# Gate and up of two row blocks as seven block products, in a kernel of a 2D spectral filter and a ReGLU

## The chip, the cores and the metric

The kernel runs on one core of a Trainium2 chip. The metric is the device time of one execution in microseconds; the time before is the median of three runs, 408.8 us (408.67 to 408.9).

## The reference

```python
x = A_x                                        # 1 x 2048 x 512, float32
xn = layernorm(x)                              # over the last axis
s = irfft2(rfft2(xn) * (w_r + 1j * w_i))       # over (2048, 512)
gate, up = xn @ W_gate, xn @ W_up              # 512 x 1376 each
g = silu((relu(gate) * up) @ W_down)           # 1376 x 512
return x + s * g
```

## The kernel before

The 2048 rows lie as 16 tiles of 128 rows by 512. Two tiles make a chunk (c or q from 0 to 7), four a row block (0 to 3); features come as 11 tiles of 128, the last one (TAIL) of 96. Every float32 operand is split into a float16 high and a float16 low part, and every product is three matmuls (PASSES: high by high, high by low, low by high).

The work has two strands. The feed-forward strand: `product` makes gate (i = 0) and up (i = 1) of one feature tile for a row block, 12 matmuls of 128x512 each; `rectify` (ACT) and `hidden` (DVE, ACT, DVE) make the float16 pair h16 from them; `down` multiplies by the down weights `wds`, and `gate` applies silu on ACT. The spectral strand is a DFT in steps: `fold`, `split` and `first_stage` (PE tile s, result through DRAM buffer A_d), then eight `fft_chunk`s (PE tiles y, xx, z, v; DVE multiplies by the filter in `tt`, POOL adds in `po` and `pf`; through DRAM buffer C_d), then `last_stage`. `finish` multiplies s by g, adds x and stores.

At the start `load_x` and `load_group` fetch the first two chunks and the gate and up weights in seven groups (`raw0` to `raw6`; in rows, raw0_0 is gate's and raw0_1 up's). `squares` sums squares of each weight tile on ACT (rows wgu,m<-raw), PE adds them over the partitions (sum, small), DVE makes scales of them (p), and `group_split` makes the float16 pairs `wgu`. Chunks 0 and 1 are normalised to `xf`, transposed on PE (head) and copied to `xT` by ACT (high) and DVE (low). Row block 0's first two features are computed in two halves, so that chunk 0 can begin before chunk 1. The down weights `wds` are scaled by the greatest of all: ACT sums their absolute values (rows wds,md<-wds), DVE takes the maximum `md`, and `greatest` sends it over the partitions by two DMAs on SP (row_md out to DRAM, rows_md back in), after which DVE makes the scales `scd`, and ACT (high) and DVE (low) split each feature's weights. No `down` product can begin before its weights are split.

`keep_busy` gives PE 79 matmuls on ones, without use, at the start. All DMAs are issued by SP. The class `Plan` sets the order on every engine: steps have costs, due times and leads (numbers at the head of the file), and a greedy list of them is written out as the program, each engine running its own in order. Operations are recorded through one helper, so all of them carry its line (L65; in the changed file L81).

## Time and profile before

| | |
|---|---|
| median of three runs | 408.8 us |
| the profiled execution, from first to last instruction | 407.1 us |
| busy: DVE, ACT, POOL | 304.0, 188.0, 46.7 us |
| DMA moved | 51.78 MB |
| the 16 DMA engines' time on the main queue | 42.5% |

The profiled execution's span is 1.7 us below the median of the runs; what lies around the span is not in the trace. Times in the profile count from the span's start. PE is the matmul engine and PEld its weight loads, which overlap the matmuls; DVE, ACT and POOL are the vector, scalar and GpSimd engines; SPq is the queue from which SP issues DMAs.

### The profile page before, as it was taken

The numbers are of one execution on the slowest core, as the hardware profiler recorded it, in microseconds if no ns is written. First come the engines' busy times: TensorE is split into PE (matmuls) and PEld (weight loads), VectorE is DVE, ScalarE is ACT, GpSimd is POOL, SyncE is SP. The second block draws the span as 40 slices with busy tenths as digits, with TensorE's granted clock in tenths as the row PEclk, the third lists the DMA queues.
The fourth block names the chain that finished last, engine by engine and source line by source line (L and its number), as shares of the span: only waits on it lengthen the run. The fifth ranks groups of instructions, "written<-read, shape, count | busy, mean of one in ns | idle before, by whom it ended". The sixth has DMA issues, their size and how long they took to land.

```text
span 407.1 us, 7606 instructions
## 1 busy us (share of the span) xinstructions
PE 401.4 (99%) x2992; PEld 211.5 (52%) x2992; DVE 304.0 (75%) x647; ACT 188.0 (46%) x358; POOL 46.7 (11%) x72
## 2 busy tenths in 40 slices
PE   8999999999999999999999999999999999999995
PEld 7864444444444445455465455546555444444555
DVE  4897986998798979706987578686792328987974
ACT  4999823743467636222355433534523336242411
POOL 0000000000000000001612032030330008040300
PEclk9999999999999999999999999999999999999999
DMA  7980002218549608690006540324201297563242
GB/s 244 403 304 1 0 2 109 54 52 208 171 152 305 172 15 209 128 291 13 2 0 191 173 144 0 100 92 149 52 2 52 61 242 182 161 185 105 103 156 103
DMA packets 36291, 51.78 MB, mean 127 GB/s; under 512 B 15840, under 2 KB 17600, under 8 KB 36256
## 3 DMA queue, kind: packets, MB, share of 16 engines
q1 hardware_dynamic: 36256, 51.31, 42.5%
q8 instruction: 23, 0.38, 0.4%
q14 instruction: 12, 0.10, 0.1%
HBM read 35.55 MB, written 12.60 MB: 118 GB/s over the span
## 4 chain that ended last, share of the span: by engine, by line
PE 97%; ACT 1%; DVE 1%; issue 0%
PE gu L65 55%; PE dn L65 27%; PE s L65 3%; PE z L65 3%; PE xx L65 3%; PE small L65 2%; PE y L65 2%; PE v L65 2%; PE dn_3b L65 1%; ACT xT L65 1%; ACT wgu L65 0%; PE head L65 0%; DVE xT L65 0%; PE sum L65 0%; DVE p L65 0%
## 5 line engine op out<-in xcount | busy, mean ns | idle before, releaser
L65 PE MATMUL gu<-xT,wgu 128*128 128x512 f16 (+1 forms) x1008 | 213.3, 369 | 0.4 <-DVE xT L65 0.4
L65 PEld LDWEIGHTS <-wgu 128*128 128x128 f16 x1008 | 97.5, 98 | 107.5 <-issue 3.5
L65 PE MATMUL dn<-wds,h 128*128 128x512 f16 (+2 forms) x528 | 115.8, 373 | 0.0
L65 PEld LDWEIGHTS <-h 128*128 128x128 f16 (+1 forms) x561 | 53.7, 98 | 57.3 <-issue 2.0
L65 DVE TENSOR_TENSOR h<-gu,r 128x512 f32<-128x512 f32 (+2 forms) x52 | 33.6, 646 | 24.2 <-PE gu L65 22.9
L65 ACT ACTIVATE h<-h 128x512 f16<-128x512 f32 (+1 forms) x44 | 27.5, 626 | 51.0 <-DVE h L65 51.0
L65 POOL TENSOR_TENSOR po<-tt,tt 128x256 f32<-128x256 f32 x16 | 14.4, 900 | 262.6 <-DVE tt L65 208.7
L65 ACT ACTIVATE r<-gu 128x512 f32<-128x512 f32 (+1 forms) x44 | 26.2, 595 | 36.5 <-PE gu L65 36.3
L65 DVE TENSOR_TENSOR h<-h,h 128x512 f16<-128x512 f32 (+1 forms) x44 | 29.7, 689 | 5.3 <-ACT h L65 5.1
L65 DVE SCALAR_TENSOR_TENSOR tt<-xsp,cw,wt 128x512 f32<-128x512 f32 x32 | 25.3, 847 | 0.0
L65 POOL TENSOR_TENSOR ae<-zz 128x128 f32<-128x128 f32 (+1 forms) x32 | 17.8, 593 | 62.8 <-ACT zz L65 47.9
L65 ACT ACTIVATE g<-dn,cdi 128x512 f32<-128x512 f32 (+1 forms) x16 | 10.6, 673 | 23.9 <-PE dn L65 23.9
L65 PE MATMUL gu<-xT,wgt 128*64 128x256 f16 (+1 forms) x144 | 17.0, 309 | 0.0
L65 DVE TENSOR_TENSOR sv<-sv,g 128x512 f32<-128x512 f32 (+1 forms) x17 | 11.2, 690 | 6.4 <-ACT g L65 6.1
L65 DVE TENSOR_TENSOR t<-v,t 128x1024 f16<-128x1024 f32 x8 | 9.8, 1219 | 7.9 <-ACT t L65 7.9
L65 DVE TENSOR_TENSOR z<-z,z 128x1024 f16<-128x1024 f32 x8 | 9.7, 1218 | 7.5 <-ACT z L65 7.5
L65 ACT ACTIVATE z<-z 128x1024 f16<-128x1024 f32 x8 | 8.2, 1024 | 15.2 <-PE z L65 15.2
L65 POOL TENSOR_TENSOR pf<-tt,tt 128x256 f32<-128x256 f32 x16 | 14.0, 888 | 7.7 <-PE gu L65 7.7
L65 ACT ACTIVATE p<-pf 128x1024 f16<-128x1024 f32 x8 | 8.4, 1056 | 13.0 <-DVE pf L65 13.0
L65 DVE SCALAR_TENSOR_TENSOR wgu<-raw,p,wgu 128x512 f16<-128x512 f32 x20 | 14.4, 745 | 0.1
L65 ACT ACTIVATE xs<-xs 128x1024 f16<-128x1024 f32 x8 | 8.3, 1052 | 12.8 <-DVE xs L65 9.3
L65 ACT ACTIVATE wgu<-raw 128x512 f16<-128x512 f32 x20 | 12.3, 619 | 3.7 <-DMA raw<-in_wg 3.7
(134 smaller groups left out, 430.6 us busy)
## 6 DMA issues: line engine op xcount, KB each, us to landing
A_d<-t SPq DMA_DIRECT2D x16, 256.0 KB, 3.3
rw<-in_wl SPq DMA_DIRECT2D x8, 512.0 KB, 5.1
wt<-in_wl SPq DMA_DIRECT2D x8, 512.0 KB, 4.8
at<-A_d SPq DMA_DIRECT2D x8, 512.0 KB, 4.9
C_d<-t SPq DMA_DIRECT2D x16, 256.0 KB, 3.3
ct<-C_d SPq DMA_DIRECT2D x16, 256.0 KB, 5.6
xt<-in_x SPq DMA_DIRECT2D x16, 256.0 KB, 4.3
out<-xt SPq DMA_DIRECT2D x15, 256.0 KB, 2.1
```

Of the source, the lines that this page charges most:

```text
L65: return lambda *args, **kw: self.tc.keep_in_program_order(f(*args, **kw))
```

## The change

Row blocks 2 and 3 take ten of the feature tiles in five pairs (PAIRS). For one pair, the 512 rows are two halves, the 512 inputs two halves, and gate and up are the two columns of a 2 by 2 block product of eight blocks; `fast_products` forms it from seven (Strassen's method, in Winograd's form). One block product is 12 matmuls of 128x256. Three accumulators A, B, C in PSUM (rows sa, sb, sc) take the products; ACT copies partial sums from A to B and from C to `back` (sk), DVE adds `back` and B into C and E (se). The hidden values follow on DVE or POOL. TAIL and blocks 0 and 1 (PLAIN) stay plain products. In all, PE has 432 instead of 912 matmuls of 128x512 for gu, and 840 of 128x256 more.

The operands of the seven products are sums. `row_sums` makes four of the normalised rows for each of the two blocks (POOL or DVE), splits them, writes them to DRAM (S_d), and transposes them back by DMA. `weight_sums` loads each pair's raw weights a second time, scales them on ACT by the kept scales (csc), makes four differences on POOL or DVE, and splits them into `wT`; one of them takes the place of up's low half in `wgu`.

Further: the transposes of chunks 2 to 7 go through DRAM too (X_d); silu's result of blocks 0 to 2 is written out to DRAM (G_d) and read back for `finish`; for chunks 0, 2, 3, 4 and 5 x is copied to the output by a DMA from DRAM to DRAM, and s by g is added to it by an accumulating DMA that POOL issues (ADDS). Statistics of chunk 2 and some normalising move to ACT. PSUM tag gu has three buffers instead of two, dn one instead of two; the pools k4, k2 and xg get smaller. All due times are replaced, and thus the order on every engine.

The diff, cut:

```diff
+PAIRS = ((0, 1), (3, 4), (5, 6), (7, 8), (2, 9))
...
-T0, DOWN, FIRST, FIRST_STEP, MID, MID_STEP, LAST, LAST_STEP = 1.2, 94.9, 53.3, 17.6, 150.3, 18.1, 292.6, 10.8
-LOADS, LOADX = [4.2, 0, 4.4, None, None, None, None], [-2.7, -0.3]
...
+T0, DOWN = 1.2, 72.63
+FIRSTS = [56.77, 70.59, 88.5, 109.16, 99.23, 144.36, 170.4, 200.62]
+LOADS, LOADX = [-28.05, -8.07, -11.28, None, None, None, None], [-2.7, -0.3]
...
+STATS, ADDS, COPIES = ['DVE', 'DVE', 'ACT', 'DVE', 'DVE', 'DVE', 'DVE', 'DVE'], ['DMA', 'DVE', 'DMA', 'DMA', 'DMA', 'DMA', 'DVE', 'DVE'], [200, 200, 200, 200, 200, 130.87, 134.53, 134.53]
-BUSY, LATE, PAIR1, PAIR2 = 79, 0.4, 0, 0
-SQUARES, HALF = 32.82, 2
+BUSY, LATE = 79, 0.4
+SQUARES, HALF = -0.132, 2
...
+ROOM = {"k4": 10, "k2": 8, "kg": 4, "cm": 3, "h16": 11, "xg": 3, "F": 2, "gu": 3, "dn": 1, "q": 4, "q4": 2, "mv": 4, "m": 4, "p": 4, "am": 1, "mid": 3}
+SUMS, TSUMS = ['POOL', 'POOL', 'POOL', 'DVE'], ['DVE', 'POOL', 'DVE', 'POOL', 'POOL']
+TPREP, TSTEP, XLEAD = 108.983, 31.324, 24.245
+PLAIN = {(1, n) for n in range(5)}
...
-    T = Plan({"k4": 12, "k2": 10, "h16": NFT, "xg": NBL + 1, "F": 2, "gu": 2, "dn": 2, "q": 4, "q4": 2, "mv": 4, "m": 4, "p": 4, "am": 1, "mid": 3})
+    T = Plan(ROOM)
...
-            SP.dma_start_transpose(xt.rearrange("p i k r -> p (i k) r"), x16().rearrange("p i h d -> p (i h d)"))
-        step("SP", 3.4, run, reads=[(f"x16_{c}", i, h) for i in range(2) for h in range(2)], 
-             writes=[(f"xT{c // 2}", j, h) for j in range(2 * (c % 2), 2 * (c % 2) + 2) for h in range(2)], kb=100)
+            SP.dma_start_transpose(xt.rearrange("p i k r -> p (i k) r"), X_d[c])
+        step("SP", .6, lambda: SP.dma_start(X_d[c], x16().rearrange("p i h d -> p (i h d)")),
+             reads=[(f"x16_{c}", i, h) for i in range(2) for h in range(2)], writes=[("X_d", c)], kb=512, due=XDUE[c])
+        step("SP", .6, run, reads=[("X_d", c)], writes=[(f"xT{c // 2}", j, h) for j in range(2 * (c % 2), 2 * (c % 2) + 2) for h in range(2)], kb=900, lead=XLEAD)
+    def row_sums(c):
+        xa, xb = (lambda k=k: T[f"xf{2 * c + k}"] for k in range(2))
+        X = [(f"xf{2 * c + k}", i) for k in range(2) for i in range(2)]
+        sx, s16 = ([f"{k}{c}_{a}" for a in range(2)] for k in ("sx", "sx16_"))
+        for a in range(2):
...
+        lo, hi = slice(0, 256), slice(256, 512)
+        eng, e, cost = (DVE, "DVE", dve(512)) if SUMS[c] == "DVE" else (POOL, "POOL", pool(512))
+        S = lambda n: T[sx[n // 2]][:, n % 2]
+        for n, op, a, b, needs in ((0, "tensor_add", lambda: xb()[:, :, lo], lambda: xb()[:, :, hi], []),
+                                   (1, "tensor_sub", lambda: S(0), lambda: xa()[:, :, lo], [(sx[0], 0)]),
+                                   (2, "tensor_sub", lambda: xa()[:, :, lo], lambda: xb()[:, :, lo], []),
+                                   (3, "tensor_sub", lambda: xa()[:, :, hi], lambda: S(1), [(sx[0], 1)])):
+            step(e, cost, lambda n=n, op=op, a=a, b=b: getattr(eng, op)(S(n), a(), b()), reads=X + needs, writes=[(sx[n // 2], n % 2)], port=True)
+        tile_of(f"xS{c}", "xg", [P, 4, 2, 4, P], F16)
+        for a in range(2):
+            halves = [(sx[a], k) for k in range(2)]
+            step("ACT", act(1024), lambda a=a: ACT.activation(T[s16[a]][:, :, :, 0, :], T[sx[a]], AF.Copy), reads=halves, writes=[(s16[a], 0)])
+            step("DVE", dve(1024), lambda a=a: DVE.tensor_sub(T[s16[a]][:, :, :, 1, :], T[sx[a]], T[s16[a]][:, :, :, 0, :]),
+                 reads=halves + [(s16[a], 0)], writes=[(s16[a], 1)], port=True)
...
+            step("SP", .6, lambda a=a, flat=flat: SP.dma_start(S_d[c][a], flat()), reads=[(s16[a], 0), (s16[a], 1)], writes=[("S_d", c, a)], kb=512,
+                 due=SDUE[c])
+            step("SP", .6, run, reads=[("S_d", c, a)], writes=[(f"xS{c}", a)], kb=900, lead=XLEAD)
...
+    def weight_sums(n, due):
+        fs = PAIRS[n]
+        raw, t16 = f"rp{n}", f"wT{n}"
+        tile_of(raw, "xg", [P, 2, 4, 2 * P], F32)
+        for i, src in enumerate((wg, wu)):
+            for j, f in enumerate(fs):
...
+                step("SP", .5, lambda i=i, j=j, of=of, o=o: SP.dma_start(T[raw][:, i, :, j * P:j * P + P], of[:, :, o:o + P]),
+                     reads=["go"], writes=[(raw, i, j)], lead=8, kb=256, due=due - 12)
+                part = lambda i=i, j=j: T[raw][:, i, :, j * P:j * P + P]
+                step("ACT", act(512) + .1, lambda part=part, f=f, i=i: ACT.activation(part(), part(), AF.Copy, scale=csc[:, i, f:f + 1]),
+                     reads=[("csc", f)], writes=[(raw, i, j)])
...
+        minus((0, 0), (1, 0), (0, 0), G + U, t1)
+        minus((1, 0), (1, 1), (1, 0), U + [t1], t3)
+        minus((1, 1), (1, 1), (0, 0), U + [t1, t3], t2)
+        minus((0, 1), (0, 1), (1, 1), G + [t2], t4)
+        for to, of, needs, k in ((slice(0, 2), lambda: T[raw][:, 0].rearrange("p (t k) f -> p t k f", t=2), [t1, t4, t2], 0),
+                                 (slice(2, 3), lambda: B(1, 1).unsqueeze(1), [t2, t4], 2)):
...
+            step("ACT", act(m), lambda to=to, of=of: ACT.activation(wT[n][:, to, 0], of(), AF.Copy), reads=needs, writes=[(t16, k)], due=due + 2)
+            step("DVE", dve(m), lambda to=to, of=of: DVE.tensor_sub(wT[n][:, to, 1], of(), wT[n][:, to, 0]), reads=needs + [(t16, k)], writes=[(t16, k + 1)], port=True, due=due + 4)
+        for j, f in enumerate(fs):
...
+            step("ACT", act(256), lambda to=to, of=of: ACT.activation(to(0), of(), AF.Copy), reads=[t3], writes=[("wgu", f, 0, 1)], due=due + 2)
+            step("DVE", dve(256), lambda to=to, of=of: DVE.tensor_sub(to(1), of(), to(0)), reads=[t3, ("wgu", f, 0, 1)], writes=[("wgu", f, 1, 1)], port=True, due=due + 4)
...
+    def fast_products(c, n):
+        fs = PAIRS[n]
+        A, B, C, back, E, r1, r2 = (f"{k}{c}_{n}" for k in ("sa", "sb", "sc", "sk", "se", "sr", "sq"))
+        for name, tag in ((A, "gu"), (B, "gu"), (C, "gu"), (back, "kg"), (E, "kg"), (r1, "kg"), (r2, "kg")):
+            tile_of(name, tag, [P, 2, 256], F32)
...
+        def mult(to, x, w, fresh, reads):
+            def run():
+                for j in range(2):
+                    for k in range(2):
+                        for p, (h, l) in enumerate(PASSES):
+                            matmul(T[to][:, j, :], w(h, k, j), x(l, k), start=fresh and j == k == p == 0, stop=j == k == 1 and p == 2, skip_group_check=True)
+            step("PE", pe(12, 256), run, reads=reads, writes=[to, "turn"], due=tick(pe(12, 256)))
+        def copy(to, of, due=None):
+            step("ACT", act(512), lambda: ACT.activation(T[to], T[of], AF.Copy), reads=[of], writes=[to], due=due)
+        def add(to):
+            step("DVE", dve(512), lambda: DVE.tensor_add(T[to], T[B], T[back]), reads=[B, back], writes=[to], due=clock[0] + 2)
+        def rect(to, of):
+            step("ACT", act(512), lambda: ACT.activation(T[to], T[of], AF.Relu, scale=2.0 ** -22), reads=[of], writes=[to], due=clock[0] + 3)
+        mult(A, rows(0, 0), plain(0, 0), True, X[0] + W[0])
+        copy(B, A)
+        mult(C, rsum(2), plain(1, 0), True, [(f"xS{c}", 1)] + W[1])
+        copy(back, C)
+        mult(B, rsum(1), summed(2), False, [(f"xS{c}", 0)] + U(2, 3))
+        mult(A, rows(0, 2), plain(0, 2), False, X[0] + W[0])
+        rect(r1, A)
+        add(C)
+        mult(B, rsum(0), summed(0), False, [(f"xS{c}", 0)] + U(0, 1))
+        mult(C, rows(1, 2), summed(1), False, X[1] + U(0, 1))
+        rect(r2, C)
+        add(E)
+        mult(B, rsum(3), plain(1, 2), False, [(f"xS{c}", 1)] + W[1])
+        step("DVE", dve(512), lambda: DVE.tensor_mul(T[r1], T[B], T[r1]), reads=[B], writes=[r1], due=clock[0] + 3)
+        e, eng, cost = (("DVE", DVE, dve), ("POOL", POOL, pool))[SECONDS[5 * c + n] == "POOL"]
+        step(e, cost(512), lambda: eng.tensor_mul(T[E], T[E], T[r2]), reads=[r2], writes=[E], due=clock[0] + 3, port=True)
+        for m, h32 in enumerate((r1, E)):
...
+            step("ACT", act(512), lambda h32=h32, h16=h16: ACT.activation(T[h16][:, 0], T[h32], AF.Copy), reads=[h32], writes=[(h16, 0)])
...
+            step(e, cost(512), lambda h32=h32, h16=h16, eng=eng: eng.tensor_sub(T[h16][:, 1], T[h32], T[h16][:, 0]), reads=[h32, (h16, 0)], writes=[(h16, 1)], port=True)
+    def ff_steps(c, lag=2):
+        for n in range(len(PAIRS)):
+            if (c, n) in PLAIN:
+                for f in PAIRS[n]:
+                    product(c, f, 0)
+                    rectify(c, f)
+                    product(c, f, 1)
+                    hidden(c, f)
+            else:
+                fast_products(c, n)
+            if n >= lag:
+                for f in PAIRS[n - lag]:
+                    down(c, f, 0)
...
+        if b < NBL - 1:
+            tile_of(g, "k2", [P, D], F32)
+            step("SP", .5, lambda: SP.dma_start(T[g], G_d[:, 2 * c + i, :]), reads=[("G_d", b, j), (sn, 2)], writes=[(g, 0)], lead=8, kb=256)
+        if ADDS[c] == "DMA":
+            to = out[:, 2 * c + i, :]
+            step("SP", .5, lambda: SP.dma_start(to, x[:, 2 * c + i, :]), writes=[("out", c, i)], lead=10, kb=512, due=COPIES[c])
+            step("DVE", dve(D), lambda: DVE.tensor_mul(T[sn][:, i, :], T[sn][:, i, :], T[g]), port=True,
+                 reads=[(g, 0), *((sn, k) for k in range(3))], writes=[(sn, 3 + i)])
+            step("POOL", 1.2, lambda: POOL.dma_start(to, T[sn][:, i, :], accum_op=ALU.add), reads=[(sn, 3 + i)], writes=[("out", c, i)], kb=512, lag=3., due=due)
+            return
...
+        for n in range(len(PAIRS)):
+            if (c, n) not in PLAIN and (c == 1 or (c - 1, n) in PLAIN):
+                weight_sums(n, TPREP + n * TSTEP)
         ff_steps(c)
```

What the order shows at three places:

The first is the start. SP's loads before (x0 and x1 are chunks 0 and 1, raw the weights of gate and up, wds those of down):

```order
L65 DMA x0_121<-in_x 128x512 x2
L65 DMA raw0_0_128<-in_wg 128x512
L65 DMA raw0_1_133<-in_wu 128x512
L65 DMA x1_148<-in_x 128x1024
L65 DMA raw1_0_152<-in_wg 128x512
L65 DMA raw1_1_163<-in_wu 128x512
L65 DMA raw2_0_171<-in_wg 128x512
L65 DMA raw2_1_178<-in_wu 128x512
L65 DMA raw3_0_190<-in_wg 128x1024
L65 DMA raw3_1_197<-in_wu 128x1024
L65 DMA wds_85<-in_wd 128x3x512
```

and with the change:

```order
L81 DMA wds_107<-in_wd 128x3x512
L81 DMA raw0_0_145<-in_wg 128x512
L81 DMA raw0_1_149<-in_wu 128x512
L81 DMA x0_153<-in_x 128x512 x2
L81 DMA wds_107<-in_wd 128x3x512
L81 DMA wds_107<-in_wd 128x2x512 x2
L81 DMA x1_200<-in_x 128x1024
L81 DMA raw2_0_216<-in_wg 128x512
L81 DMA raw2_1_224<-in_wu 128x512
L81 DMA raw1_0_207<-in_wg 128x512
L81 DMA raw1_1_249<-in_wu 128x512
L81 DMA raw3_0_256<-in_wg 128x1024
```

The loads of the down weights came after those of x and of four weight groups; now one stands first, and three more ahead of x1. On ACT before, between the first squares and the transposed rows of chunk 0 (xT0):

```order
L65 ACTIVATE wgu0_77,m0_168<-raw0_0_128 128x512
L65 ACTIVATE q0_166<-q0_166 128x2
L65 ACTIVATE wgu0_77,m0_168<-raw0_1_133 128x512
L65 ACTIVATE xf0_201<-x0_121,q0_166 128x512
L65 ACTIVATE wgu0_77<-raw0_0_128,p0_210 128x512
L65 ACTIVATE xT0_233<-head0_214 128x512 x2
L65 ACTIVATE wgu1_78,m1_251<-raw1_0_152 128x512
L65 ACTIVATE wgu1_78,m1_251<-raw1_1_163 128x512
L65 ACTIVATE wgu0_77<-raw0_1_133,p0_210 128x512
```

and with the change:

```order
L81 ACTIVATE wgu0_94,m0_181<-raw0_0_145 128x512
L81 ACTIVATE wgu0_94,m0_181<-raw0_1_149 128x512
L81 ACTIVATE wds_107,md_112<-wds_107 128x512 x2
L81 ACTIVATE q0_229<-q0_229 128x2
L81 ACTIVATE wds_107,md_112<-wds_107 128x512
L81 ACTIVATE wgu0_94<-raw0_0_145,p0_232 128x512
L81 ACTIVATE wgu0_94<-raw0_1_149,p0_232 128x512
L81 ACTIVATE wds_107,md_112<-wds_107 128x512
L81 ACTIVATE xf0_281<-x0_153,q0_229 128x512
L81 ACTIVATE wds_107,md_112<-wds_107 128x512
L81 ACTIVATE xT0_298<-head0_286 128x512 x2
L81 ACTIVATE wds_107,md_112<-wds_107 128x512 x2
```

Five sums over the down weights now stand ahead of xT0, and three more follow ahead of the second chunk's xT0 (not shown).

The second is DVE behind the maximum of the down weights; xs16_1 is the operand of chunk 1's first stage s1_1, which on PE stood ahead of the tail product and now stands among the first down products. Before:

```order
L65 TENSOR_REDUCE max_md_105<-rows_md_104 128x1
L65 TENSOR_SCALAR pd_106<-max_md_105 128x1
L65 TENSOR_SCALAR pd_106<-pd_106 128x1 x2
L65 TENSOR_SCALAR cdi_87<-pd_106 128x1
L65 TENSOR_SCALAR scd_91<-rho_86,pd_106 128x11
L65 TENSOR_TENSOR xs16_1_684<-xs1_570,xs16_1_684 128x2x512
L65 TENSOR_TENSOR h32_0_8_843<-gu0_8_1_803,r0_8_817 128x512
L65 SCALAR_TENSOR_TENSOR wds_85<-wds_85,scd_91 128x512
```

and with the change, from nine rows behind the maximum:

```order
L81 TENSOR_TENSOR h16_0_8_909<-h32_0_8_905,h16_0_8_909 128x512
L81 TENSOR_TENSOR xs1_726<-ee1_718 128x2x65
L81 TENSOR_TENSOR xs1_726<-ee1_718 128x2x64
L81 SCALAR_TENSOR_TENSOR wds_107<-wds_107,scd_114 128x512
L81 TENSOR_TENSOR xs1_726<-ee1_718 128x2x64
L81 TENSOR_TENSOR xs1_726<-ee1_718 128x2x63
L81 TENSOR_SCALAR st2_794<-st2_794 128x2
L81 BN_STATS st3_940<-x3_722 128x6
L81 BN_AGGR mv3_942<-st3_940 128x2
L81 SCALAR_TENSOR_TENSOR wds_107<-wds_107,scd_114 128x512
L81 TENSOR_TENSOR h32_0_9_961<-gu0_9_1_914,r0_9_928 128x512
L81 TENSOR_TENSOR xs16_1_944<-xs1_726,xs16_1_944 128x2x512
```

The low part of xs16_1 came directly behind scd, from sums xs1 made long before; now four of xs1's sums, two splits of down weights and other work stand between.

The third is the first pair of seven products in block 2 (sb2_0 and sc2_0 its accumulators, sk2_0 the copy), on DVE:

```order
L81 SCALAR_TENSOR_TENSOR tt0_0_2516<-xsp_0_2496,cw_110,wt_0_1854 128x512
L81 SCALAR_TENSOR_TENSOR tt1_0_2534<-xsp_0_2496,cw_110,wt_0_1854 128x512
L81 SCALAR_TENSOR_TENSOR tt2_0_2536<-xsp_0_2496,cw_110,wt_0_1854 128x512
L81 SCALAR_TENSOR_TENSOR tt3_0_2553<-xsp_0_2496,cw_110,wt_0_1854 128x512
L81 TENSOR_TENSOR xsp_1_2555<-xx1_2519,xo1_2551 128x256
L81 TENSOR_TENSOR xsp_1_2555<-xx1_2519,xo1_2551 128x4x32
L81 TENSOR_TENSOR xsp_1_2555<-xo1_2551,xx1_2519 128x4x32
L81 SCALAR_TENSOR_TENSOR tt0_1_2577<-xsp_1_2555,cw_110,wt_1_2037 128x512
L81 TENSOR_TENSOR sc2_0_2538<-sb2_0_2532,sk2_0_2574 128x512
L81 COPY zd_138<-zb_2484 128x2
L81 TENSOR_SCALAR zd_138<-zb_2484 128x2
```

The addition into sc2_0, which the next product into sb2_0 waits for, stands behind filter multiplications of spectral chunks 0 and 1.

223 lines of the change are left out of this document (145 added, 78 removed).

## The prediction

> **What bounds the kernel now.** I read the page's busy time first, then the time by stretches of 20 us, then the chain of waits.
>
> ```profile
> PE 401.4 (99%) x2992; PEld 211.5 (52%) x2992; DVE 304.0 (75%) x647; ACT 188.0 (46%) x358; POOL 46.7 (11%) x72
> ```
>
> In the stretches the numbers are the length, then busy time and instructions of PE, PEld, DVE, ACT and POOL, then the granted clock, the DMA engines' share and GB/s:
>
> ```profile
> 0.00:20.00 20.00, 18.78 (x150) 15.67 (x151) 13.22 (x46) 13.55 (x34) 1.00 (x8) 1.00 0.89 322
> 20.00:40.00 20.00, 19.61 (x119) 11.40 (x117) 17.59 (x47) 19.15 (x53) 0.00 (x0) 1.00 0.47 162
> 60.00:80.00 20.00, 20.00 (x152) 9.97 (x151) 15.06 (x30) 10.95 (x18) 0.00 (x0) 1.00 0.26 83
> ```
>
> PE is full from 20 us on; its busy 18.78 us before that hold the useless matmuls on ones. The chain (start, length, what) says the same: from 20.83 on it runs on PE with no other engine between, to 403.03; behind that comes a short tail.
>
> ```profile
> 20.83 18.24 PE gu L65 x107
> ...
> 41.80 0.34 PE sum L65 x4
> ...
> 68.06 1.44 PE s L65 x48
> 69.50 4.13 PE gu L65 x36
> 73.63 27.30 PE dn L65 x126
> ...
> 103.12 15.54 PE gu L65 x72
> ...
> 187.47 1.31 PE xx L65 x12
> ...
> 403.03 0.02 issue
> 403.06 0.48 ACT g L65
> 403.56 0.43 DVE sv L65
> 404.02 0.42 DVE xt L65
> ```
>
> So work taken from PE is worth its full time as long as PE stays fed, and whatever makes PE wait costs its full time. Two things follow: price PE's work, then look for where PE will wait. The tail behind PE keeps its form, since the last block's last products, gate and additions are as before, and counts as zero.
>
> **PE's work.** A 512-wide matmul takes 15.54/72 = 0.216 us, a 256-wide one 1.31/12 = 0.109 us (rows at 103.12 and 187.47). The change takes 480 of the first (103.6 us) and adds 840 of the second (91.7 us): **-11.9 us**. Every row of weight loads speaks for the 0.109:
>
> ```profile
> L65 PEld LDWEIGHTS <-wgu 128*128 128x128 f16 x1008 | 97.5, 98 | 107.5 <-issue 3.5
> ```
>
> 98 ns stay below 109, so a new weight load per 256-wide matmul is still covered, with little left.
>
> **The start.** In the second half of the first features, at 20.83, PE becomes full. What lies ahead of it:
>
> ```profile
> GB/s 244 403 304 1 0 2 109 54 52 208 171 152 305 172 15 209 128 291 13 2 0 191 173 144 0 100 92 149 52 2 52 61 242 182 161 185 105 103 156 103
> ...
> 0.73 0.86 SPq L65 DMA_DIRECT2D x<-in_x  x2
> 3.49 0.69 DVE L65 BATCH_NORM_STATS2 st<-x 128x6 f32<-128x512 f32 x1 [2.47 <-DMA x<-in_x]
> 5.97 0.63 ACT L65 ACTIVATE wgu<-raw 128x512 f16<-128x512 f32 x1 [3.75 <-DMA raw<-in_wg]
> 9.14 0.69 DVE L65 BATCH_NORM_STATS2 st<-x 128x6 f32<-128x512 f32 x1
> 19.49 1.29 DVE L65 TENSOR_TENSOR xT<-head,xT 128x512 f16<-128x512 f32 x2 [0.81 <-ACT xT L65]
> 20.83 11.33 PE L65 MATMUL gu<-xT,wgu 128*128 128x256 f16 x75 [0.39 <-DVE xT L65]
> ```
>
> The first row is the rate in 40 slices of 10.2 us: 2.5 MB by 10.2 us, 6.6 MB by 20.4. x0 landed at 3.5, raw0 at 6.0. In the new order of SP's loads 768 KB of down weights stand ahead of x0, and 1,792 KB more ahead of x1. By these slices the first 2.6 MB (down to the second load of wds) are in at some 10.5 us, x1 (4.2 MB) at 14.4, raw1 at 17.0, raw3 at 19.6. On ACT, which was busy 13.55 us of the first 20 (first stretch) and began its squares at 5.97, stand eight more sums over wds:
>
> ```profile
> L65 ACT ACTIVATE wds<-wds 128x512 f32<-128x512 f32 x10 | 6.2, 617 | 0.0
> L65 ACT ACTIVATE wgu<-raw,p 128x512 f16<-128x512 f32 x12 | 8.1, 714 | 0.6 <-DVE p L65 0.6
> L65 ACT ACTIVATE xf<-x,q 128x512 f32<-128x512 f32 x2 | 1.6, 814 | 0.4 <-DVE q L65 0.4
> L65 ACT ACTIVATE xT<-head 128x512 f16<-128x512 f32 x4 | 2.2, 589 | 0.9 <-PE head L65 0.9
> ```
>
> ACT's row up to the second xT0 is now: 19 squares or sums of 0.62 (11.8 us), four splits of 0.71 (2.8), two xf (1.6), three of four xT0 copies (1.8): 18 us. Without any wait it ends at 24, and DVE's two low copies (1.29) bring PE's second half to 25.1, that is 4.3 late: the lower bound, since raw0 can't land earlier than before. With the waits that the bytes above make (for chunk 0's statistics to 9.7, the second and third loads of wds at 10.5 and 13.1) I get 26.3; if loads that are under way together all land with the last byte among them, raw3 and raw4 come at 20 to 23.5, and the half begins at 29. I take **+6.0** (4.3 to 8). PE has no other work to put there, for the 79 matmuls on ones now run out ahead of the first transposes.
>
> That idle time has a price of its own if PE begins slowly after it, as it does at launch:
>
> ```profile
> 1.05 6.42 PE L65 MATMUL small<-ones 128*128 128x256 f16 x38 [1.05 <-DVE md L65]
> 9.33 2.78 PE L65 MATMUL small<-ones 128*128 128x256 f16 x24
> ```
>
> The first 38 matmuls on ones took 0.169 us each, later ones 0.116: 2.0 us lost over 38. The granted clock reads 1.00 in the first stretch all the same, so the rows don't say why, and the sum leaves it out; it is a rival below. The Trainium skill ("TensorE: Matmul & The Clock Gate", the section on the HAM clock gate) has a reason: an idle window of about 3.4 us halves PE's clock until it has been busy for as long. By it the sum would be some 1.7 us more.
>
> **The down weights.** Before, the first down product found its weights ready:
>
> ```profile
> 50.03 0.16 DVE L65 TENSOR_REDUCE md<-md 128x1 f32<-128x11 f32 x1
> 64.45 0.29 DVE L65 TENSOR_REDUCE max_md<-rows_md 128x1 f32<-128x128 f32 x1 [4.16 <-DMA rows_md<-row_md]
> 65.34 0.23 DVE L65 TENSOR_SCALAR scd<-rho,pd 128x11 f32<-128x11 f32 x1
> 65.48 1.22 DVE L65 TENSOR_TENSOR xs<-xs,xs 128x1024 f16<-128x1024 f32 x1
> 67.22 0.74 DVE L65 SCALAR_TENSOR_TENSOR wds<-wds,scd 128x512 f16<-128x512 f32 x1
> ...
> SPq L65 <- DMA row_md<-md: 8.9, 1, 8.9
> ```
>
> From md to its maximum are 14.4 us of two DMAs, whatever PE does. Reckon from the second half's start S (20.83). md was at S+29.2. In the new order three products of 2.6 us more stand ahead of the sums of the last weight groups, at S+28.8 rather than S+21; fewer DVE operations stand behind them, and I get md at S+32, the maximum at S+46.4, scd at S+47.4. Behind it on DVE come one hidden product, four sums into xs1, the statistics, two splits of wds, and ACT, held until scd, makes two more splits and xs16_1's high part ahead of xs16_1's low part: S+54.8. PE gets to s1_1 at S+53: 1.8 us of wait. Then the low halves of features 5 to 7, between the normalising work on DVE, come some 1.5 late for their products. I take **+3.5** (0 to 8.5: nothing if DVE is 2 us faster in both places; 5 more if the sums take DVE 8 us to md, as in the trace of before).
>
> **The seven products.** Each of them waits for the one before in its accumulator: B must be read by DVE (add into C, then into E) before the next product adds to it, and one product of 1.31 us covers that. Alone, that holds: a copy on ACT or an add on DVE is 0.6 to 0.7 us. But DVE works in order, and ahead of an add stand rows like these, the first of them four at a time:
>
> ```profile
> L65 DVE SCALAR_TENSOR_TENSOR tt<-xsp,cw,wt 128x512 f32<-128x512 f32 x32 | 25.3, 847 | 0.0
> L65 DVE TENSOR_TENSOR h<-gu,r 128x512 f32<-128x512 f32 x40 | 27.5, 687 | 21.9 <-PE gu L65 20.8 <-ACT junk L65 0.5 <-ACT r L65 0.3
> L65 DVE SCALAR_TENSOR_TENSOR wgu<-raw,p,wgu 128x512 f16<-128x512 f32 x20 | 14.4, 745 | 0.1
> L65 POOL TENSOR_TENSOR po<-tt,tt 128x256 f32<-128x256 f32 x16 | 14.4, 900 | 262.6 <-DVE tt L65 208.7 <-issue 23.8 <-ACT t L65 14.5
> ```
>
> For the first pair (the order's third piece) I follow it through: four tt (3.4 us), xsp of chunk 1 (1.0), a fifth tt (0.85) and the add (0.69) end 0.9 us behind the point at which PE wants it, and the add into E, behind the corner terms, some 0.2 later than wanted. Six of the ten pairs run beside spectral stages; at 0.7 each that makes **+4** (0 to 10, the latter 1 us for each of ten). This takes the place of no wait: in block 2 PE was full.
>
> POOL's thirty new operations of 128x512 (row sums, weight differences, second hidden products) cost, by the 900 ns for half the width, 1.5 to 1.8 us each, about 50 us. They have no place on PE's path of their own, as the results are wanted much later, but they touch DVE: the same form of DVE operation takes 745 ns at the start, where POOL rests, and 847 where POOL works beside it, 3.3 us over 32. The Trainium skill ("SBUF — State Buffer", on the shared port pair) has it that a POOL operation and a DVE operation with two operands in SBUF exclude each other for a whole instruction. The 100 ns in the rows agree in sign; by the rule in full most of POOL's new time would be added to DVE's.
>
> **The sum.** 407.1 - 11.9 + 6.0 + 3.5 + 4 = 408.7 of span; with the 1.7 us by which the median of the runs lies above the profiled execution, **410.4 us**, 0.4% slower. DMA bytes (row sums, transposes through DRAM, weights loaded again, about half as much again as 51.8 MB) are counted as zero: the engines' share was 0.26 to 0.47 in the later stretches, and what waits for them is planned microseconds ahead. The other replaced due times, too, count as zero for want of a row.
>
> **The rivals.** First, faster: the start is late by its lower bound, DVE reaches scd in time and the adds are covered. Then 407.1 - 11.9 + 4.3 = 399.5, with 1.7 401.2; with one of the two small terms, 404. For it: PE never waits after 20 us in the trace of before, where the same planner placed the work; DVE has a quarter of its time free. Against it: each of the three waits has its place in the new order. Chance 0.36.
>
> Second, slower by DVE and POOL as the bound in block 2. POOL's 50 us at the share that the rows show (3.3 of its 28 us) cost DVE 6; if half of POOL's time there is added to DVE's, DVE's work in the 90 us of block 2, by my count of its rows some 74 us, becomes longer than PE's, and PE follows DVE: 6 to 10 us more, 416 to 420. It decides from 16 us of lost DVE time in block 2. It is what the skill's port rule, in full force, would do. For it, the 847; against it, the rows of POOL lie between DVE's and most DVE rows read PSUM. Chance 0.13.
>
> Third, PE slow after the idle start as at launch: 2.0 us for each of one or two idle spells, 412.4 to 414.4. Chance 0.04. Fourth, 256-wide matmuls held by weight loads, so that the change does less than it says: at 0.12 us each, 9 us more, 419. Against it stand 1.31 us for twelve such matmuls. Chance 0.02.
>
> **The numbers.** The forecast as worked has 0.45, with its own range 407 to 415. Less than 0.2% of 408.8, 0.8 us to either side, can't be told from no change here. Faster than 408.0 has the first rival and a little of the forecast's lower edge: 0.37; 408.0 to 409.6 has 0.08; slower 0.55. The range is 400 to 418: below it only a start that costs nothing, above it the worst of the second and fourth rivals.
>
> **What would show it.** PE's first continuous stretch should begin near 27 us and not at 20.8; a gap on PE near s1_1 with xs16_1 or wds as what ended it, of 2 to 5 us; ten to twenty gaps of under 1 us ahead of sb and sc, ended by DVE; sa, sb and sc at 1.31 us for twelve; no slow matmuls behind the start. The prediction is wrong if PE is full from 25 us on with the three waits missing, or if DVE in the stretch of block 2 is at 95% or more.

## The result, and the profile after

The changed kernel takes **430.4 us** (median of four runs, 429.4 to 433.3) against 408.9 (408.7 to 409.2) beside it on the same chip: 1.054 times as long, interval 1.050 to 1.057. The forecast was 410.4, range 400 to 418: the sign was right, the size far off. The profiled execution was the longest of the four, 433.3 us with a span of 431.5.

The page's busy times and the granted clock in 40 slices:

```profile
PE 401.8 (93%) x3352; PEld 250.8 (58%) x3352; DVE 345.1 (80%) x711; ACT 230.3 (53%) x432; POOL 82.7 (19%) x95
PEclk9889999999999999969899998999999999999999
```

PE is busy as long as before (401.8 us against 401.4), though its work shrank by 11.9 us: some of its time is stretched, and the clock row's 8s and the 6 say where. Its idle time grew from 5.7 to 29.7 us. What it waited for (total, times, longest):

```profile
PE sb L81 <- DVE sc L81: 5.4, 4, 2.1
PE s L81 <- DVE h L81: 4.3, 1, 4.3
PE y L81 <- DMA at<-A_d: 4.0, 1, 4.0
PE gu L81 <- ACT xT L81: 2.3, 2, 1.2
PE gu L81 <- DVE xT L81: 2.1, 2, 1.1
PE gu L81 <- DVE wgu L81: 1.9, 2, 1.2
PE gu L81 <- ACT r L81: 1.8, 1, 1.8
PE dn L81 <- DVE h L81: 1.0, 1, 1.0
```

Three gu lines belong to the start, sb to the seven products, s and y to one place between row blocks 1 and 2. First the start, in PE's timeline:

```profile
15.86 0.27 PE L81 MATMUL gu<-xT,wgu 128*128 128x256 f16 x1 [1.17 <-ACT xT L81]
17.18 4.23 PE L81 MATMUL gu<-xT,wgu 128*128 128x256 f16 x23 [1.05 <-DVE xT L81]
22.99 0.39 PE L81 MATMUL gu<-xT,wgu 128*128 128x256 f16 x2 [1.24 <-DVE wgu L81]
30.21 0.27 PE L81 MATMUL gu<-xT,wgu 128*128 128x256 f16 x1 [1.17 <-ACT xT L81]
31.53 4.64 PE L81 MATMUL gu<-xT,wgu 128*128 128x256 f16 x41 [1.05 <-DVE xT L81]
```

The second half, at 20.83 before, begins at 31.53. The 23 matmuls at 17.18 take 4.23 us, 0.18 each instead of 0.109. The stretches (length; busy time and count of PE, PEld, DVE, ACT, POOL; granted clock; DMA share; GB/s) say why:

```profile
18.00:20.00 2.00, 2.00 (x11) 1.40 (x10) 1.89 (x7) 2.00 (x8) 0.00 (x0) 0.50 1.03 346
24.00:26.00 2.00, 1.95 (x10) 1.40 (x11) 1.90 (x11) 1.80 (x4) 0.00 (x0) 0.50 0.37 43
...
186.00:188.00 2.00, 1.66 (x25) 1.03 (x26) 1.97 (x4) 0.67 (x2) 0.00 (x0) 0.50 0.78 71
188.00:190.00 2.00, 2.00 (x6) 0.70 (x5) 0.92 (x3) 1.04 (x2) 0.00 (x0) 0.50 1.26 262
190.00:192.00 2.00, 2.00 (x9) 0.72 (x8) 1.97 (x4) 1.18 (x3) 0.00 (x0) 0.73 1.03 222
...
212.00:214.00 2.00, 2.00 (x80) 2.00 (x77) 1.10 (x2) 1.54 (x3) 1.84 (x3) 0.50 1.04 419
214.00:216.00 2.00, 2.00 (x16) 0.91 (x12) 2.00 (x3) 0.09 (x1) 1.17 (x1) 0.76 1.01 410
```

After idle time PE works at half clock for some microseconds. Now the boundary in the timelines, PE first (idle time before a row stands in brackets):

```profile
186.34 1.50 PE L81 MATMUL s<-xs,cR 64*64 64x257 f16 x24 [4.28 <-DVE h L81]
...
211.05 0.23 PE L81 MATMUL y<-cm,at 64*128 64x64 f16 x4 [4.00 <-DMA at<-A_d]
```

DVE ahead of the first of these:

```profile
181.49 0.68 DVE L81 TENSOR_TENSOR rp<-rp 128x512 f32<-128x512 f32 x1
184.58 0.24 DVE L81 COPY wt<-spw 128x4 f32<-128x4 f32 x2 [2.42 <-DMA wt<-E_d]
184.73 1.56 DVE L81 TENSOR_TENSOR h<-gu,r 64x256 f32<-64x256 f32 x3
```

A copy of a few elements waits 2.42 us for a transfer (`wt` from E_d, issued at 173.98), ahead of the hidden operations whose PSUM buffer the last s stage needs. SP ahead of the second:

```profile
174.67 5.21 SPq L81 DMA_TRANSPOSE xT<-X_d  x1
...
184.74 5.60 SPq L81 DMA_TRANSPOSE xT<-X_d  x1
190.39 5.05 SPq L81 DMA_TRANSPOSE xS<-S_d  x2
...
196.21 4.23 SPq L81 DMA_DIRECT2D A_d<-t  x4
...
204.56 1.11 SPq L81 DMA_DIRECT2D at<-A_d  x2
```

Read from the bottom: y's input `at` needs all of A_d, and A_d's last four stores stand in SP's queue behind transposes that held it 15.9 of the 21 us to 195.4. Before, y began at 180.8.

The seven products themselves, in their worst pair:

```profile
255.98 1.48 PE L81 MATMUL sb<-xS,wT 128*128 128x256 f16 x12
257.30 1.47 PE L81 MATMUL sa<-xT,wgu 128*128 128x256 f16 x12
258.61 0.81 PE L81 MATMUL dn<-wds,h 128*128 128x512 f16 x3
261.48 1.53 PE L81 MATMUL sb<-xS,wT 128*128 128x256 f16 x12 [2.05 <-DVE sc L81]
```

From start to start twelve matmuls take 1.31 us, as priced. Beside the forecast's terms, in us of span:

| term | forecast | measured |
|---|---|---|
| PE's matmuls | -11.9 | -11.9 (1.31 for twelve) |
| start, 20.83 to 31.53 | +6.0 | +10.7, half clock included |
| down weights | +3.5 | +1.8 (one wait, for r) |
| seven products | +4 | +7.4: waits 5.7, half clock 1.7 |
| boundary of block 2 | 0 | +12.2: waits 8.3, half clock 3.9 |
| waits for h and others | 0 | +1.5 |
| not assigned | | +2.7 |
| span | 408.7 | 431.5 |

A half clock is counted as one minus the granted clock over the stretch that PE was busy; for the boundary that is 0.83 + 1.0 + 0.54 behind s and 1.0 + 0.48 behind y. The tail behind PE kept its 4.1 us. The table counts PE's waits and slow time in the profiled execution; it doesn't say what the time would fall by without one of them. The wait put to the down weights stands ahead of s1_1: ACT stood still for `scd` until 76.83, and r came at 84.21, behind splits of `wds` and other work.

### The profile page after: what moved, and what is told of

The parts are those of the page before. It is cut to its first block, busy times and chain, and to the rows that moved or that the text cites. A ratio compares the mean times of both kernels' runs of the same rounds, so it can differ in the third digit from the quotient of the medians.

```text
span 431.5 us, 8605 instructions
## 1 busy us (share of the span) xinstructions
PE 401.8 (93%) x3352; PEld 250.8 (58%) x3352; DVE 345.1 (80%) x711; ACT 230.3 (53%) x432; POOL 82.7 (19%) x95
## 5 line engine op out<-in xcount | busy, mean ns | idle before, releaser
L81 PE MATMUL gu<-xT,wgu 128*128 128x512 f16 (+1 forms) x528 | 109.6, 368 | 6.7 <-ACT xT L81 2.3
L81 PEld LDWEIGHTS <-wT 128*128 128x128 f16 x360 | 35.2, 99 | 13.3 <-issue 8.3
L81 PE MATMUL sb<-xS,wT 128*128 128x256 f16 x240 | 29.6, 273 | 5.4 <-DVE sc L81 5.4
L81 PE MATMUL sa<-xT,wgu 128*128 128x256 f16 x240 | 29.5, 273 | 0.0
L81 ACT ACTIVATE h<-h 128x512 f16<-128x512 f32 (+1 forms) x24 | 14.9, 624 | 26.9 <-DVE h L81 26.8
L81 POOL TENSOR_TENSOR rp<-rp 128x512 f32<-128x512 f32 x12 | 17.1, 1423 | 52.1 <-ACT rp L81 51.5
L81 DVE TENSOR_TENSOR h<-gu,r 128x512 f32<-128x512 f32 (+2 forms) x32 | 19.8, 619 | 4.9 <-PE gu L81 3.4
L81 ACT ACTIVATE rp<-rp,csc 128x512 f32<-128x512 f32 x20 | 13.6, 714 | 5.4 <-DMA rp<-in_wg 5.3
L81 PE MATMUL sc<-xT,wT 128*128 128x256 f16 x120 | 16.0, 287 | 0.0
L81 DVE TENSOR_TENSOR sv<-ye 128x510 f32<-128x510 f32 x16 | 15.2, 989 | 0.1
L81 PE MATMUL sb<-xS,wgu 128*128 128x256 f16 x120 | 15.2, 277 | 0.0
```

What stands on the lines that cost most here:

```text
L81: return lambda *args, **kw: self.tc.keep_in_program_order(f(*args, **kw))
```

## The experiments

Theory A: the late start is the main price, and it and each wait come back one for one. Theory B: a strand beside PE (DVE in order, SP's queue, the transfers) sets the pace later, so a gain at one place returns as a wait at another.

**The start, and plain products.** Three kernels from the changed one, and one from the kernel before.

```diff
e_start:       -LOADS ... [-28.05, -8.07, -11.28, ...  SQUARES = -0.132
               +LOADS ... [4.2, 0, 4.4, ...            SQUARES = 32.82
               +  reads=["raw3_0"] in both loads of load_down
e_busy:        -BUSY = 79
               +BUSY = 170
e_plain:       -PLAIN = {(1, n) for n in range(5)}
               +PLAIN = {(c, n) for c in range(1, NBL) for n in range(5)}
e_before_late: before, with the changed kernel's LOADS, SQUARES, DOWN, and lead=90 in load_down
```

> The changed kernel with the loads of the start in the order of before: x0, raw0, x1 and the weight groups 1 to 4 ahead of the down weights, the sums over the down weights later on ACT. Theory A (the late start is lost time): PE's unbroken stretch begins at 20 to 22 us and not at 31.5, no slow clock ahead of it, and the time falls by 9 to 11 us, to 419 to 421. Rival (DVE, busy 19 of 20 us from 40 to 180, sets the pace of block 1, so that PE merely waits for it later): the start is early but the time falls by less than 4 us, to 427 or more, and new waits of PE for DVE stand between 80 and 180 us.

> The changed kernel with 170 instead of 79 matmuls on ones; the further ones go into the planned gaps of PE in the first 25 us. Theory A (part of the late start is PE at half clock after idle gaps, granted clock 0.50 at 18 to 20 and 24 to 26 us): the clock reads 1.00 throughout the start, the second half begins some 3 us sooner, at 28 to 29, and the time falls by 2 to 3 us. Rival (ACT, DVE and the loads alone set the start): the second half begins at 31 to 32 as before and the time stays within 1 us.

> The changed kernel with all five pairs of blocks 2 and 3 as plain products: no row sums, no weight sums, no second load of weights, no seven products; the start, the transposes of x through DRAM and the accumulating DMAs stay. PE's work grows by 11.9 us. Theory A (the sums and what they need in DVE, in SP's queue and in transposes cost more than the 11.9 us): the two waits at 182 to 186 and 207 to 211 us and the slow clock behind them (12 us) and the waits between the seven products (5.7 us, with 1.7 of slow clock) go, and the time falls by 4 to 8 us, to 422 to 426. Rival (the waits come from the new due times, the transposes of x and the start, not from the seven products): the waits at 182 to 211 stay, and the time is 435 to 442.

> The kernel before, with only the loads at the start in the changed kernel's order: all of the down weights but the first 768 KB ahead of x1, the first 768 KB ahead of all, and the sums over them early on ACT. Theory A (the late start costs its full length in either kernel): PE's unbroken stretch begins at 29 to 32 us and the time grows by 8 to 11 us, to 417 to 420. Rival (an earlier maximum of the down weights or slack later takes it back): 409 to 413.

e_start measured 436.0 us (1.067, 1.065 to 1.070), e_busy 437.3 (1.068, 1.064 to 1.072), e_plain 425.4 (1.041, 1.037 to 1.046), e_before_late 425.1 (1.038, 1.033 to 1.043). In e_start the second half came 7.3 us earlier, and the time rose by 5.6 where theory A had it fall by 9 to 11. PE was done at 422.9 there and DVE worked on for some 10 us:

```profile
400.00:420.00 20.00, 19.84 (x133) 10.98 (x132) 17.37 (x34) 5.95 (x18) 7.72 (x11) 1.00 0.74 174
420.00:436.00 16.00, 2.89 (x27) 2.35 (x24) 12.19 (x22) 1.36 (x4) 6.03 (x8) 0.73 0.78 194
```

e_busy kept the clock at 1.00 through the start and brought the second half to 29.86, 1.7 us sooner; it lost more later (5.31 us ahead of an sb at 393.6). All plain products are 5 us faster than seven, with 12 us more of PE work, and without the two waits between row blocks 1 and 2. e_before_late doesn't price a late start, because its start is hardly late. PE's unbroken stretch begins at 22.49, not at the expected 29 to 32:

```profile
22.49 11.89 PE L65 MATMUL gu<-xT,wgu 128*128 128x256 f16 x84
```

That is 1.7 us behind the 20.83 of before, while the time grew by 16. Most of it is lost later, such as 3.22 us ahead of y at 189.4 and the half clock behind that wait. In all four kernels the planner also wrote a new order on every engine; what that alone can do is seen below.

**The plain form early, one block alone, transposes from SBUF, no accumulating DMAs.**

```diff
e_plain_early: e_plain and e_start's edits together
e_only2:       +PLAIN = {(c, n) for c in (1, 3) for n in range(5)}
e_direct:      -SP.dma_start_transpose(xt, X_d[c])    and xS from S_d; their stores
               +SP.dma_start_transpose(xt, x16())     step cost 3.4 as before
e_adds:        +ADDS = ['DVE'] * 8
```

> The changed kernel with plain products in all row blocks (no sums, no seven products) and with the early start of the kernel before (its loads and square due times, weight loads of the down products behind the first gate and up loads). The plain form with the late start measured 425.4 us, 16.5 above before. If the late start (with the half clock behind its gaps) is the plain form's only loss: 408 to 412 us, the clock 1.00 from about 26 us on. If the other replaced due times, buffer numbers, G_d stores and accumulating DMAs cost time of their own, as a late end behind the tensor engine did in the early-start run with seven products: 415 us or more, with a wait over 2 us behind 110 us or a tail over 6 us behind the last matmul.

> The changed kernel with seven products in the third row block only; the fourth has plain products (no row sums for it either). PE work goes up by 6 us against the changed kernel. If the seven products' price sits at the boundary of the second and third blocks and in the third block's pair waits (theory): the fourth block's seven products are a gain or nothing, so 430 to 436 us. If the price is spread over both blocks, or sits at the end, where VectorE is busy 20 of 20 us: half-way between plain (425.4) and changed (430.4) or below, 423 to 428 us, and VectorE busy under 18 of 20 us in the last 40 us.

> The changed kernel with its DMA transposes reading the 16-bit halves in on-chip memory, as before, instead of a copy of them in DRAM (10 stores of 512 KB less). Theory: SyncE's queue, held 16 of 21 us by transposes at 174 to 195 us, makes the waits of 4.28 and 4.00 us ahead of s and y and the half clock behind them; if reading from DRAM is what holds the queue, each transpose takes 2 to 3.4 us there and 8 to 12 us go: 418 to 423 us. Rival: a transpose holds the queue as long whatever it reads, or VectorE (19 to 20 of 20 us) sets the pace there: within 3 us of 430.

> The changed kernel with all final additions on VectorE, no accumulating DMAs (10 of 16 output tiles had them). Theory: they sit behind the last products and cost little; VectorE gets 10 additions of about 0.6 us back, GpSimd loses 8.9 us of DMA issues, sv and ye rows go back towards 701 and 475 ns: 429 to 433 us, the tail behind the last matmul 4 to 6 us. Rival: the accumulating DMAs and their 10 DRAM copies are a main price (contention in the second half): 425 us or less. Other rival: VectorE is full at the end and the additions make it last: 435 us or more with a tail over 8 us.

e_plain_early: 421.5 us (1.033, 1.029 to 1.036). So even with plain products and an early start the changed program loses 12.7 us against before. At the start PE is full from 24.05 on (20.83 before), and later it is idle ahead of

```profile
77.56 1.50 PE L81 MATMUL gu<-xT,wgt 128*64 128x256 f16 x24 [1.50 <-ACT r L81]
172.41 1.50 PE L81 MATMUL gu<-xT,wgt 128*64 128x256 f16 x24 [1.42 <-ACT r L81]
364.64 2.75 PE L81 MATMUL gu<-xT,wgu 128*128 128x512 f16 x12 [0.84 <-DVE h L81]
```

where PE had not waited before. e_only2 (its fourth block works with up weights that the sums have partly replaced): 442.9 (1.083, 1.081 to 1.085), slower than both its neighbours: neither guess held. e_direct: 462.7 (1.130, 1.127 to 1.134), outside both its ranges; its transposes held SP's queue 2.6 to 5.4 us a row all the same, so reading from SBUF doesn't free the queue. e_adds: 433.2 (1.063, 1.056 to 1.069), 0.2 above its 429 to 433 and far from the 425 at which the accumulating DMAs would have been a main price.

**Sums later, less work for DVE, a copy moved.** Theory B in a sharper form is theory C of these expectations; its rival D puts SP's queue in DVE's place.

```diff
e_only3:       +PLAIN = {(c, n) for c in (1, 2) for n in range(5)};  TPREP = 200
e_only3_early: the same, with e_start's edits
e_lows:        - step("DVE", ...) of wT's, wgu's and x16's low halves in the sums
e_fill:        - step("DVE", .3, fill, reads=["spw"], writes=[wtn])
               + step("DVE", .3, fill, reads=["spw", atn], writes=[wtn])
```

> The changed kernel with seven products in the last row block only, and the sums of the weights due behind 200 us instead of 109 us. Theory C: the time is a strand that runs through VectorE. The second stage of the filter (y) cannot begin before all eight first stages, which VectorE, full from 40 to 200 us with the sums in its queue, made late (y_0 at 211 us; 201 in the plain form); the last stage begins 155 us behind y_0 (s2_0 at 366; 352 plain), and needs 62 us or more behind that. Without the sums ahead of y_0: y_0 at 198 to 203, s2_0 at 348 to 355, 418 to 423 us, below the plain form's 425.4 by about the 6 us of matmuls saved. Rival: the seven products lose more by their own waits and sums than their matmuls save, wherever they stand: 426 us or more although y_0 comes at 200.

> The same with the early start. Plain products with the early start measured 421.5 us (y_0 at 192). Theory C: y_0 at 190 to 195, 414 to 418 us. Rival (seven products lose by themselves): 422 us or more.

> The changed kernel without the low halves of the sums: VectorE's subtractions for them (20 us in all) are left out, zeros or old values stand in their place, so that the output is not the reference's. Theory C: VectorE has 20 us less ahead of 290 us, some 12 of them ahead of y_0: y_0 at 200 to 205, 420 to 425 us. Rival D: SyncE's queue (transposes of 2.5 to 5.6 us each) makes y_0 late: y_0 stays at 208 to 212 and the time within 3 us of 430.

> The changed kernel with the filling of the filter's weights tile (VectorE's copy that waited 2.42 us for its transfer at 182 us, ahead of the hidden tile for which the tensor engine waited 4.28 us) moved behind the arrival of the second stage's input. If that copy made the wait: the 4.28 us and half of the half clock behind it go, 424 to 428 us. If VectorE was late there anyway: the wait stays at 2 us or more and the time within 2 us of 430.

446.2 us (1.090, 1.085 to 1.095), 437.5 (1.063, 1.057 to 1.069), 446.8 (1.092, 1.089 to 1.096) and 454.8 (1.113, 1.110 to 1.116). The first two lie in the open ranges of their rival (426 or more, 422 or more), the others where no theory put them. In e_only3 the y stage began at 208.1, not at the 200 that both theories had. e_fill cut the wait ahead of s to 2.35, and a new one of 16.34 us stood at its end, ahead of an sb.

What they share with all runs above is that the planner wrote a new order on every engine. In e_fill one added dependency, with the same work, moved the time by 24 us, far more than the parts in question. So none of the runs so far prices what it changed.

**The same order.** The next four keep every step, engine, cost and dependency in the plan, so that each engine's order stays the changed kernel's; only what an instruction does is made short. (e_fix_loads also fills what isn't loaded with constants: 5.89 us on DVE from 1.18 on, while DVE waits for x0.)

```diff
e_fix_turn:  -SP.dma_start_transpose(...)          +SP.dma_start(...), same bytes
e_fix_lows:  -DVE.tensor_sub(low halves of sums)   +one column, or DVE.memset
e_fix_loads: -SP.dma_start(wdr[:, ...])            +SP.dma_start(wdr[0:32, ...])
e_fix_three: e_fix_turn and e_fix_lows, and
             -DVE.tensor_copy(wt()[:, i, :, 0], spw[:, 0, i, :])
             +DVE.tensor_copy(spw[:, 1, i, :], spw[:, 0, i, :])
```

> The changed kernel in the same order on every engine, with ordinary transfers of the same bytes in place of its 14 DMA transposes (the products get untransposed data, so the output is not the reference's). If transposes holding SyncE's queue made the boundary's waits (4.28 us ahead of s, 4.00 ahead of y, about 4 of half clock): y_0 at 200 to 206 instead of 211, 420 to 425 us. If VectorE was late there on its own: y_0 within 2 us of 211, 428 to 431 us.

> The changed kernel in the same order on every engine, with VectorE's subtractions for the low halves of the sums shrunk to a column or a fill with zeros (about 18 us less on VectorE; the sums are then taken without their low halves, so the output is not the reference's). If VectorE's load makes the waits: y_0 at 200 to 206, 419 to 425 us. If VectorE only waits for others there (transfers): y_0 within 2 us of 211, 427 to 431 us.

> The changed kernel in the same order on every engine, with the first five loads (weights of the down products) carrying 32 of 128 partitions, 2.1 MB less, and constants filled in for the rest at the very start (so the output is not the reference's). At the 390 to 420 GB/s of the start, 2.1 MB are 5 us. If the late start is paid in full: second half of the start at 25 to 28 us instead of 31.5, 422 to 426 us. If later work sets the pace whatever the start does, as the early start with a new order suggested: 428 to 431 us, with larger waits at 180 to 215 us.

> The changed kernel in the same order on every engine, with ordinary transfers for transposes, the low halves of the sums shrunk, and the fill of the filter's weights (which waited 2.42 us for its transfer at 182 us) written to another place (output not the reference's). All three suspects of the boundary at once: if they are its causes, both boundary waits and their half clock go, and the pair waits shrink by half: 413 to 420 us. If something else sets the pace (the first stage's chain itself): 424 us or more.

e_fix_turn (there are ten transposes, not fourteen): **425.5 us** (1.041, 1.036 to 1.046), 4.9 less than the changed kernel. SP's queue there:

```profile
184.03 0.42 SPq L81 DMA_DIRECT2D xT<-X_d  x1
184.51 0.90 SPq L81 DMA_DIRECT2D xS<-S_d  x2
...
188.48 3.43 SPq L81 DMA_DIRECT2D A_d<-t  x4
...
196.23 2.56 SPq L81 DMA_DIRECT2D at<-A_d  x2
```

And its PE:

```profile
185.58 0.85 PE L81 MATMUL s<-xs,cR 64*64 64x257 f16 x24 [3.77 <-DVE h L81]
...
205.65 0.23 PE L81 MATMUL y<-cm,at 64*128 64x64 f16 x4
```

In these rows the queue is held 0.4 to 0.5 us per transfer instead of 2.5 to 5.6, A_d's stores go out 7.7 us sooner, and the wait ahead of y is gone. From the first of the stores to DVE's copy of `at` are 14.9 us in the changed kernel and 13.6 here, so it is mainly the freed queue that counts, and not faster transfers. The wait ahead of s stays: the transposes don't make it. e_fix_lows: 428.7 (1.045, 1.039 to 1.051), its executions overlapping with those of the changed kernel. Its wait ahead of s fell from 4.28 to 0.3, the one ahead of y rose from 4.00 to 4.72, and the seven products' waits stayed at 5.5. This doesn't show that DVE's load made the wait ahead of s. DVE was ready for the copy at 182.1 to 182.2 in both kernels; s began 1.5 us sooner (184.83), as the copy's transfer came sooner (0.97 us of wait for 2.42), and PE itself arrived 2.5 us later, behind a longer half clock at the start. e_fix_three: 426.3 (1.040, 1.035 to 1.046), above its 413 to 420. Both boundary waits are gone but for 2.1 us, and y begins 9.5 us earlier. DVE reached the copy's place at 178.7 there, against 181.9 in e_fix_turn, and the copy no longer waited; which of the two the s stage needed isn't separated. Then, on PE and in the stretch behind:

```profile
201.53 0.23 PE L81 MATMUL y<-cm,at 64*128 64x64 f16 x4 [2.10 <-DMA at<-A_d]
...
219.73 1.77 PE L81 MATMUL sb<-xS,wT 128*128 128x256 f16 x12 [2.47 <-DVE sc L81]
```

```profile
222.00:224.00 2.00, 2.00 (x12) 1.16 (x10) 1.93 (x3) 0.00 (x0) 1.20 (x2) 0.50 0.18 50
```

The first sb waits twice as long (1.23 in the changed kernel), with half clock behind it; the second y stage then begins at 223.99, where e_fix_turn had it (223.96). The gain over e_fix_turn was given back whole, and a second gap of 2.06 us, ahead of an sb at 253.66, was followed by half clock, where e_fix_turn kept 1.00. e_fix_loads: 432.7 (1.057, 1.053 to 1.061): with 2.1 MB less the second half began at 29.96, not 25 to 28. The other kernels of this order had it between 29.2 and 32.7 by how long the half clock lasted, so these bytes aren't what makes the start late. (x0's statistics began at 7.42, hardly sooner than the 7.57 of the changed kernel.) The rows that end the start's waits are ACT's and DVE's.

**Another queue, and the down weights.**

```diff
e_turn_act:   -SP.dma_start_transpose(...)    +ACT.dma_start_transpose(...), same order
e_plain_down: e_plain_early with DOWN = 94.9
```

> The changed kernel in the same order on every engine, with its DMA transposes issued from ScalarE's queue instead of SyncE's, at the same places of the order. If a held SyncE queue was the cost: the 4.0 us wait ahead of y goes as with ordinary transfers (425.5 us). But ScalarE then stands still for each store's landing and 2 to 6 us of each transpose, and the tensor engine waits for its copies: by the 35 us that transposes held SyncE's queue, more new waits on ACT than the 4 us won: 430 to 445 us. If a transpose's landing, not the queue, made y late: y_0 stays at 211.

> The changed kernel with plain products, the early start, and the down weights due at 94.9 us as in the kernel before (72.63 in the changed one). Without this it measured 421.5, with waits of 1.50, 1.42, 0.84 and 0.71 us for ScalarE's r and VectorE's h. If the earlier down weights make the 1.50 us wait and some lateness behind it: 416 to 420 us, that wait gone. If not: within 2 us of 421.5.

e_turn_act: 439.2 us (1.070, 1.062 to 1.077; the profiled execution was the fastest, 433.6). The wait ahead of y went, but not because y's input came sooner: A_d's last stores went out at 195.90 (196.21 in the changed kernel), since s came late, and PE itself came to y later than the 211.05 of the changed kernel:

```profile
212.46 0.23 PE L81 MATMUL y<-cm,at 64*128 64x64 f16 x4
```

So this run doesn't decide between the held queue and a late landing; for the held queue stand the rows of e_fix_turn. What it does show is that now ACT stands at the transpose, and r comes behind it:

```profile
184.20 4.95 ACTq L81 DMA_TRANSPOSE xT<-X_d  x1
...
189.20 0.59 ACT L81 ACTIVATE r<-gu 96x512 f32<-96x512 f32 x1 [3.90 <-issue]
```

DVE waits for r, and PE for DVE, in their timelines:

```profile
189.82 1.56 DVE L81 TENSOR_TENSOR h<-gu,r 64x256 f32<-64x256 f32 x3 [4.87 <-ACT r L81]
```

```profile
191.44 1.50 PE L81 MATMUL s<-xs,cR 64*64 64x257 f16 x24 [8.96 <-DVE h L81]
```

e_plain_down: 421.1 (1.029, 1.027 to 1.031), no different from e_plain_early, with a wait of 1.69 at the same place: in the plain form the earlier down weights are not its cause. No version was found that beats the kernel before.

## Why the prediction was wrong

**PE's work**: right, to the row; a new weight load for each 256-wide matmul stays covered, so the fourth rival falls.

**The failed step** is the sentence that counted DMA as zero ("what waits for them is planned microseconds ahead") and, with it, "the other replaced due times, too, count as zero for want of a row". At one place PE lost 12.2 us to waits and half clock, more than half of the 22.8 us between the forecast span and the measured one. I had judged the transfers by the DMA engines' share; what counted ahead of y was the time that the issue holds its queue. e_fix_turn shows this half (4.0 us of wait; 4.9 of time, for all ten transposes). Of the 4.28 us ahead of s, 2.42 are the copy's wait for a transfer; the rest may be DVE's load, and no run separates it. With both halves taken away (e_fix_three) the time fell by only 4.2 us, so the price of the boundary is shown for the y half alone. The trace of before had rows that warned: its six transposes held SP's queue for 16.3 us already. The change makes ten and lowers their cost in the plan from 3.4 us each to 0.6; in the trace they held the queue for 35.4 us.

**The start**: the mechanism was right (ACT's squares and sums over the down weights, idle PE), and the size wrong, 10.7 for 6.0. About 3 us of PE's time there are the half clock; bytes were the wrong reason for the rest, as e_fix_loads shows. The lower bound of 25.1 was also added up 0.2 short (5.97, 18.0 and 1.29 make 25.3). What the late start costs in time isn't shown: no run in the same order begins early.

**The slow PE after idle time**, left out of the sum and put at 2.0 us a spell with a chance of 0.04, was real: some 3 us at the start, 3.9 at the boundary, 1.7 behind one pair. The Trainium skill's rule on the clock gate, cited there, had the sign right; the launch row alone made me weigh it too little, and I did not ask how many idle spells the change would make.

**The down weights** were over-sized (1.8 for 3.5). Their mechanism came out: scd at 76.56, 45.0 us behind the second half's start where I had 47.4, and s1_1 at 54.7 where I had 54.8. That the 1.8 are theirs is read from ACT's rows; e_plain_down, in another order, has such a wait without them. **The seven products** were under-sized (7.4 for 4; in waits alone 5.7). Both lie inside their bounds. The waits stand ahead of sb and are ended by DVE, as foretold, though five and not ten to twenty.

**The second rival** (DVE the bound in block 2) came nearer than its 0.13 says, in another place. DVE was not full in block 2 (at most 18.95 of 20 us) but ahead of it and at the end:

```profile
120.00:140.00 20.00, 20.00 (x134) 9.21 (x132) 19.80 (x31) 13.02 (x23) 7.33 (x5) 1.00 0.65 193
380.00:400.00 20.00, 18.80 (x175) 13.98 (x174) 20.00 (x27) 7.43 (x20) 9.27 (x14) 1.00 0.77 176
```

One reading behind this rival was wrong. The rows of 745 and 847 ns are not the same form: the first writes float16, the second float32, and the second kept its 846 ns in the changed kernel with POOL busy for 82.7 us instead of 46.7. The row that did grow is sv<-ye, from 701 to 989 ns.

What stays open: why the seven-product kernel with an early start is slower than with a late one (its order is another, so the 5.6 us are not the start's), most of the 12.7 us that the plain form with an early start loses, and the 2.7 us not assigned. That DVE's queue carries the strand is argued from its full stretches and from what e_fix_three gave back, not shown. No run in the same order came below 425.5, so most of the 21.5 us by which the change is slower are counted in rows and not shown by an experiment.

## What to carry to other kernels

In a program whose order is written out by a planner, a transfer's price is the time that its issue holds a queue, and what stands behind it there: read that from the queue's rows before counting DMA as hidden. To price one part of such a program, keep the order and shorten the one instruction; letting the planner write a new order moved this kernel by 24 us where the work was the same (e_fill) and told little. When an engine that was full gets idle spells, count the slow clock behind each as well, and expect a wait that is removed to come back at the next thing that the same in-order queue makes late.
